# Linear attention and an ELU feed-forward on one core: batch 0 prepared in chunks of two heads, and six feature tiles open in the first product

## The chip, the cores and the metric

One core of a Trainium2 chip runs the whole program in one launch. The metric is the device time of the kernel in microseconds (us), the median over several runs. The engines named below: TensorE (PE; its weight loads are PEld), VectorE (DVE), ScalarE (ACT), GpSimd (POOL) and SyncE (SP). SP, ACT and POOL also issue DMAs[...].

## The reference

```
q, k, v: (8 batches, 8 heads, 576 rows, 64)  fp32;  g_norm: (64,)
kv  = einsum('bhsd,bhse->bhde', k, v)
out = einsum('bhsd,bhde->bhse', q, kv)
rms = sqrt(mean(out * out, axis=-1) + 1e-6)
att = out / rms * g_norm
x   = att.transpose(0, 2, 1, 3).reshape(4608, 512)
h   = x @ w_in                                # w_in  (512, 2048)
g   = where(h > 0, h, exp(min(h, 0)) - 1)
return g @ w_out                              # w_out (2048, 512), result (4608, 512) fp32
```

## The kernel before, in words

**Tiles.** The 4608 token rows are cut into nine tiles T of 512 rows. A tile's input to the feed-forward is `xT`: 128 partitions, four rows c (KC = 4) of 512 tokens. Row c, here called chunk c, is two heads; c = 2l + u, where l is the half of the partitions and u the step in which it is prepared. For one tile the first product makes 16 feature tiles of 128 (`h_ps`, two in a pair i = 0 to 7, each a sum over the four c), ELU turns them into `gT`, and the second product adds the 16 features f for four groups j of 128 tokens (`o_ps`). All matmuls are in bf16. `w_in_sb` and `w_out_sb` stay in SBUF for the whole run.

**ELU of a pair.** ACT takes Exp of the PSUM pair. DVE takes the minimum with 1 and subtracts 1, and then either takes the maximum with the PSUM pair itself, or, where ACT has also written Relu of the pair into SBUF (`relu=True`), adds that. In the first case the PSUM pair is free after DVE's pass, in the second after ACT's.

**Attention of tile 0** (the part that the diff touches). q is turned by TensorE (`turned_q`, L174) and copied to `qT`; `kv_mm` (L156) sums k and v over the rows and `kv_out` copies the result to `kv_sb`; `y_mm` (L189) gives the attention output with tokens along the free axis; ACT squares it, `mean_mm` (L199) spreads the mean over the partitions, `inv_t` takes Ln and Exp (L208, L209), and `scale_t` (L212) writes the row of `xT`. The class `Turned` does that for one u, so for two chunks at a time.

**Order.** The schedule is manual: each engine runs its instructions in the order in which the program states them. Pools give PSUM: the pairs A and B (two banks each), and two single banks each of the kinds "m" and "x"; a new tile of a kind waits until the old one is read. `idle(n)` issues n matmuls of zeros whose result nobody reads.

**The start before.** SP loads q, k and v of batch 0 in fp32, first both chunks of u = 0, then of u = 1 (six loads; the last, v of u = 1, goes into the buffer of the first q and is issued when that is cast). DVE, ACT and, for u = 1, POOL cast them to bf16 (`first_cast`). POOL's own loads begin after its casts: w_in tiles 0 to 4 in two loads (rows c = 0 and 2, then 1 and 3), its tiles 5 to 8, 9 to 12 and 13 to 15, w_out in four quarters of four f, and between these q, k, v of batches 1 and 2. At most eight of POOL's loads are under way; a further one waits for the one eight places earlier to land.

The early first product (L581) opens five feature tiles (pairs 0 and 1 and the first half of pair 2): c = 0 and 2 when u = 0 is ready, then c = 1 and 3; the other half of pair 2 follows. Pairs 3 to 7 are the regular `mm1` (L378), in "m", B, A, "x", "m"; Relu goes to ACT for pairs 2 and 6. Then the second product of tile 0 (L399) goes feature by feature over all four j, and batch 1 is prepared between its features: `mm2_all(0, 1)`, kv of batch 1 for u = 0, f = 1 and 2, q turned, f = 3 and 4, y, f = 5, means, f = 6 to 9, then the same for u = 1. w_out's third quarter is used from f = 8 on.

Of the kernel before, what the change touches and what calls it, by code (L numbers as in the profile page):

```python
# [8 lines left out]
FP32 = mybir.dt.float32  # L9
# [7 lines left out]
def kernel(  # L17
# [90 lines left out]
    def copy_on(eng, out_, in_):  # L108
        if eng is nc.scalar:
            nc.scalar.copy(out_, in_)  # L110
        else:
            eng.tensor_copy(out=out_, in_=in_)

    def load_w_in(fs, cs=slice(0, KC)):
        cols = slice(fs.start * P, fs.stop * P)
        nc.gpsimd.dma_start(  # L116
            out=w_in_sb[:, cs, cols], in_=moe_w_in.rearrange("(c p) f -> p c f", p=P)[:, cs, cols]
        )
# [24 lines left out]
    def qT_tile(b):  # L143
        qT[b] = attp.tile([P, 2, 2, RK, 64], BF16, name="qT", tag="qT", bufs=3)
        return qT[b]

    def x_tile(T):
        xT[T] = attp.tile([P, KC, G], BF16, name="xT", tag="xT")
        return xT[T]

    def kv_mm(b, kv_ps, u):
        for j in range(RK):
            for s in range(2):
                rows = slice(s * 64, s * 64 + 64)
                for l in range(2):
                    nc.tensor.matmul(  # L156
                        kv_ps[s][l * 64 : l * 64 + 64, u * 64 : u * 64 + 64],
                        lhsT=bf["k", b][rows, 2 * l + u, j, :],
                        rhs=bf["v", b][rows, 2 * l + u, j, :],
                        start=(j == 0),  # L160
                        stop=(j == RK - 1),
                    )
# [8 lines left out]
    def q_t_mm(b, u, js, dst):  # L171
        for n, j in enumerate(js):
            for l in range(2):
                nc.tensor.transpose(  # L174
                    dst[l * 64 : l * 64 + 64, n * P : n * P + P], bf["q", b][:, 2 * l + u, j, :], ident
                )

    def q_t_out(b, u, eng, src, js):
        copy_on(eng, qT[b][:, :, u, js, :], src.rearrange("p (j s r) -> p s j r", s=2, r=64))

    def y_mm(T, u, ps, ns=slice(0, 8)):

        n = ns.start
        while n < ns.stop:
            b, j = slot_of(T, n)
            m = min(ns.stop - n, RK - j)
            for l in range(2):
# [273 lines left out]

    first = {}

    def first_load(name, u, st):
        first[name, u] = st
        load(st, name, 0, slice(u, 4, 2), nc.sync)

    def first_tile(name):  # L470
        return stage.tile([P, 2, RK, D], FP32, name=f"first_{name}", tag=f"first_{name}")

    def first_cast(name, u, eng, js):
        copy_on(eng, bf[name, 0][:, u::2, js, :], first[name, u][:, :, js, :])

    low, high = slice(0, 5), slice(5, 9)
    for name in "qkv":
        bf[name, 0] = qkvp.tile([P, 4, RK, D], BF16, name=f"{name}_bf", tag=name)
        first_load(name, 0, first_tile(name))
    more = stage.tile([P, 4, RK, D], FP32, name="st_q", tag="q")  # L480
    for name, half in (("q", 0), ("k", 2)):
        first_load(name, 1, more[:, half : half + 2])
# [6 lines left out]
    nc.vector.memset(zeros, 0.0)  # L489
    nc.vector.memset(eps_col, 1e-6)  # L490
    nc.vector.memset(one, 1.0)  # L491
    nc.vector.memset(ones, 0.0)
    for l in range(2):
        nc.vector.memset(ones[l * 64 : l * 64 + 64, l * 64 : l * 64 + 64], 1.0 / D)

    idle_ps = pair("B", "idle_ps")

    def idle(n, ps=idle_ps[:, 0, :]):
        for _ in range(n):
            nc.tensor.matmul(ps, lhsT=zeros[:, 0:P], rhs=zeros, start=True, stop=True)  # L500

    def turned_q(b, u, tag):

        ps = as_bf16(single(tag, "qt_ps"))
        q_t_mm(b, u, range(8), ps)
        return ps

    qT_tile(0)
    x_tile(0)
    g_ps = pair("A", "g_ps")  # L510
    idle(9)
    nc.tensor.transpose(g_ps[:, 0, 0:1], g_row.rearrange("o l e -> o (l e)"), one)
    nc.vector.tensor_copy(out=g_col, in_=g_ps[:, 0, 0:1])
    first_cast("q", 0, V, low)
    first_cast("q", 0, A, high)
    first_load("v", 1, first_tile("q"))
    ps = turned_q(0, 0, "m")
    idle(10)
    q_t_out(0, 0, V, ps, slice(0, 8))
    first_cast("k", 0, A, high)  # L520
    first_cast("k", 0, V, low)
    first_cast("v", 0, V, low)
    first_cast("v", 0, A, high)
    kv_ps = [single("x", "kv_ps") for _ in range(2)]
    kv_mm(0, kv_ps, 0)
    idle(2)
    kv_out(0, kv_ps, 0, (V, A))
    first_cast("q", 1, V, low)
    first_cast("q", 1, Q, high)
    load_w_in(slice(0, 5), slice(0, KC, 2))  # L530
    first_cast("k", 1, Q, high)
    load_w_in(slice(0, 5), slice(1, KC, 2))
    first_cast("v", 1, Q, high)
    for lo, hi in ((5, 9), (9, 13), (13, 16)):
        load_w_in(slice(lo, hi))
    load_w_out(0)
    for name in "qkv":
# [8 lines left out]
            fetch(name, 2, u)  # L546
    fetch_ahead(3)
    cast_q(3)
    n0, n1 = Turned(0, 0), Turned(0, 1)
    y_ps = pair("A", "y_ps")  # L550
    n0.product([y_ps[:, l, :] for l in range(2)])
    for l in range(2):
        n0.square(l)
    ps = turned_q(0, 1, "m")
    q_t_out(0, 1, V, ps, slice(0, 8))
    first_cast("k", 1, V, low)
    first_cast("v", 1, V, low)
    idle(1)
    for l in range(2):
        n0.sums(l, single("x", "mean"))  # L560
        n0.inv(l)
    idle(7)
    kv_ps = pair("B", "kv_ps")
    kv_ps = [kv_ps[:, s, :] for s in range(2)]
    kv_mm(0, kv_ps, 1)
    kv_out(0, kv_ps, 1, (V, A))
    n0.scale(0)
    n0.scale(1)
    y_ps = [single("m", "y_ps") for _ in range(2)]
    idle(2, y_ps[0])  # L570
    n1.product(y_ps)
    for l in range(2):
        n1.square(l)
    g_tile(0)
    h0, h1 = pair("B", "h_ps"), pair("A", "h_ps")
    mean, h2 = single("x", "mean"), [single("x", "h_ps"), None]

    def early(h, i, a, cs):

        for c in cs:  # L580
            nc.tensor.matmul(  # L581
                h[a] if isinstance(h, list) else h[:, a, :],
                lhsT=w_in_sb[:, c, (2 * i + a) * P : (2 * i + a) * P + P],
                rhs=xT[0][:, c, :],
                start=(c == 0),
                stop=(c == KC - 1),
            )

    for a in range(2):
        early(h0, 0, a, (0,))  # L590
    n1.sums(0, mean)
    n1.inv(0)
    n1.scale(0)
    for a in range(2):
        early(h0, 0, a, (2,))
    for a in range(2):
        early(h1, 1, a, (0, 2))
    n1.sums(1, mean)
    n1.inv(1)
    n1.scale(1)  # L600
    early(h2, 2, 0, (0, 2))
    for c in (1, 3):
        for h, i, a in ((h0, 0, 0), (h0, 0, 1), (h1, 1, 0), (h1, 1, 1), (h2, 2, 0)):
            early(h, i, a, (c,))
    elu(0, 0, h0, False)()
    elu(0, 1, h1, False)()
    h2[1] = single("x", "h_ps")
    early(h2, 2, 1, (0, 2, 1, 3))
    elu(0, 2, h2, True)()
    for i, tag in zip(range(3, 8), "mBAxm"):  # L610
        mm1(0, i, tag, tag == "x")()

# [9 lines left out]

    x_tile(1)
    qT_tile(1)
    mm2_all(0, 1)
    for u in range(2):
        n = Turned(1, u)
        kv_ps = [single("x", "kv_ps") for _ in range(2)]  # L630
# [152 lines left out]
```

## Time and profile before

| | |
|---|---|
| median of 7 runs | 294.5 us (294.18 to 295.16) |
| the profiled execution | 294.84 us, of which the span from the first to the last instruction is 293.0 us |
| TensorE busy | 282.5 us, 96% of the span |
| DVE, ACT, POOL busy | 167.0, 142.1, 44.7 us |
| second product (L399), 560 matmuls of 512 columns | 130.7 us |
| first product, regular (L378), 552 such matmuls | 128.9 us |
| loads from memory | 36.70 MB |
| first regular matmul of the first product (L378) | at 21.93 us |
| matmuls of f = 8 of tile 0's second product | from 41.86 us |

A busy share is an average over stages: TensorE is full for most of the run, and the diff touches only the first 50 us, so those are read by themselves. In the profile a line "A <- B: 0.9, 1, 0.9" among the waits says that A waited for B for 0.9 us in total, once, 0.9 us at most. The chain of waits follows the work that ended last backwards; a DMA in it stands with the time from issue to landing. Stage rows give the busy time of each engine, the clock granted to TensorE, the share of the 16 DMA engines in use (it can exceed 1, as packets overlap), and the bytes written per time: a load that casts to bf16 reads twice what it writes.

### The profile page before, as it was taken

The page shows a single profiled execution, that of the slowest core. Times are in us where ns is not written, and L with a number is a line of the kernel's source. Part 1 is how long each engine was busy: PE and PEld are TensorE (multiplying, and loading weights), DVE is VectorE, ACT ScalarE, POOL GpSimd, SP SyncE. Part 2 cuts the span into 40 slices and gives each one's busy share as a digit, 9 for nine tenths or more (in the row PEclk, how much of TensorE's full clock was granted, in tenths as well). Part 3 has the DMA queues.
Part 4 walks back from the last instruction along what each step waited for, and adds up shares of the span by engine and source line. Part 5 has one row for each costly group of instructions (what it writes and reads, how often), then busy time and mean ns, then how long its engine had stood idle before and what let it go on. Part 6 is the DMA issues. An engine that isn't in the chain of part 4 may idle for free.

```text
span 293.0 us, 5198 instructions
## 1 busy us (share of the span) xinstructions
PE 282.5 (96%) x2152; PEld 129.9 (44%) x2152; DVE 167.0 (57%) x221; ACT 142.1 (48%) x210; POOL 44.7 (15%) x79
## 2 busy tenths in 40 slices
PE   7989889998999999999999999999999999999994
PEld 2434434443444444444444444444444444444443
DVE  2539723578258756774577557755775677444600
ACT  3678346678555525542554255425542554244311
POOL 0673332303300012403300330000000000000000
PEclk9999999999999999999999999999999999999999
DMA  7999999996911189968953995362331214020222
GB/s 254 280 175 206 207 205 207 316 234 192 185 34 36 27 139 245 201 88 177 254 114 71 174 255 125 63 128 72 38 81 27 72 38 104 4 74 0 72 72 74
DMA packets 46236, 38.95 MB, mean 133 GB/s; under 512 B 26372, under 2 KB 38916, under 8 KB 46212
## 3 DMA queue, kind: packets, MB, share of 16 engines
q0 software_dynamic: 14144, 19.53, 34.4%
q1 hardware_dynamic: 31664, 18.55, 29.0%
q10 hardware_dynamic: 404, 0.53, 0.5%
q8 instruction: 17, 0.28, 0.4%
q14 instruction: 7, 0.06, 0.1%
HBM read 36.70 MB, written 9.44 MB: 157 GB/s over the span
## 4 chain that ended last, share of the span: by engine, by line
PE 78%; DMA 13%; DVE 4%; ACT 2%; POOL 1%; issue 1%; DVEq 0%; SPq 0%
PE o_ps L399 37%; PE h_ps L378 35%; DMA w_out_sb<-in_moe_w_out_dram 9%; DMA xT<-xs 2%; DMA first_q<-in_v_dram 2%; DVE gT L362 2%; PE at L250 1%; PE idle_ps L500 1%; PE at L156 1%; PE o_ps L436 1%; ACT elu_e L350 1%; DVE elu_e L358 1%; POOL w_in_sb L116 1%; DVE xT L212 0%; PE qt_ps L174 0%
## 5 line engine op out<-in xcount | busy, mean ns | idle before, releaser
L399 PE MATMUL o_ps<-w_out_sb,gT 128*128 128x512 bf16 x560 | 130.7, 379 | 1.4 <-DMA w_out_sb<-in_moe_w_out_dram 0.9
L378 PE MATMUL h_ps<-xT,w_in_sb 128*128 128x512 bf16 x552 | 128.9, 379 | 1.0 <-DVE gT L362 0.8
L350 ACT ACTIVATE elu_e<-h_ps 128x1024 bf16<-128x1024 f32 (+1 forms) x77 | 73.9, 972 | 92.7 <-PE h_ps L378 89.9
L362 DVE TENSOR_TENSOR gT<-elu_e,h_ps 128x1024 bf16<-128x1024 bf16 (+1 forms) x73 | 85.6, 1177 | 7.3
L399 PEld LDWEIGHTS <-gT 128*128 128x128 bf16 x560 | 54.3, 98 | 67.6 <-issue 3.1
L378 PEld LDWEIGHTS <-w_in_sb 128*128 128x128 bf16 x552 | 52.4, 98 | 62.8 <-issue 2.1
L358 DVE TENSOR_SCALAR elu_e<-elu_e 128x1024 bf16<-128x1024 bf16 x72 | 31.5, 437 | 68.6 <-ACT elu_e L350 68.4
L415 ACT COPY o_sb<-o_ps 128x512 f32<-128x512 f32 x32 | 18.5, 588 | 18.8 <-PE o_ps L399 18.7
L103 POOL CAST q_bf<-st_q 128x384 bf16<-128x384 f32 x30 | 14.4, 530 | 28.8 <-DMA st_q<-in_q_dram 28.8
L283 DVE TENSOR_REDUCE ss<-sq 128x16 f32<-128x1024 bf16 x12 | 14.6, 1219 | 4.9 <-ACT sq L277 4.9
L212 DVE SCALAR_TENSOR_TENSOR xT<-y_ps,g_col,rT 128x512 bf16<-128x512 f32 x12 | 8.9, 749 | 15.0 <-ACT rT L209 15.0
L299 DVE TENSOR_TENSOR xs<-at,ss 128x1024 bf16<-128x1024 f32 x12 | 14.6, 1217 | 0.0
L277 ACT ACTIVATE sq<-at 128x1024 bf16<-128x1024 f32 x12 | 12.3, 1028 | 1.0 <-PE at L250 1.0
L339 POOL COPY gate<-qT 1x32 bf16<-1x32 bf16 x4 | 0.8, 202 | 72.6 <-DMA qT<-q_bf 72.6
L229 ACT ACTIVATE sq<-y_ps 128x512 bf16<-128x512 f32 x12 | 6.5, 595 | 7.8 <-PE y_ps L189 7.8
L500 PE MATMUL idle_ps<-zeros 128*128 128x512 bf16 x29 | 9.0, 458 | 1.2 <-DVE one L491 1.2
L208 ACT ACTIVATE rT<-mean,eps_col 128x512 f32<-128x512 f32 x12 | 8.2, 683 | 1.7 <-PE mean L199 1.5
L156 PEld LDWEIGHTS <-k_bf 64*64 64x64 bf16 x576 | 5.7, 107 | 5.7 <-issue 5.2
L209 ACT ACTIVATE rT<-rT 128x512 f32<-128x512 f32 x12 | 7.6, 630 | 0.4
L90 POOL DMA_DIRECT2D k_bf<-in_k_dram x9 | 6.6, 738 | 5.6 <-DMA w_in_sb<-in_moe_w_in_dram 1.8
L90 POOL DMA_DIRECT2D v_bf<-in_v_dram x9 | 6.7, 743 | 4.2 <-DMA w_out_sb<-in_moe_w_out_dram 1.8
L312 DVE TENSOR_SCALAR xT<-xT,g_col 128x1024 bf16<-128x1024 bf16 x12 | 5.8, 479 | 2.7 <-DMA xT<-xs 2.7
(59 smaller groups left out, 97.6 us busy)
## 6 DMA issues: line engine op xcount, KB each, us to landing
out_dram<-o_sb SPq DMA_DIRECT2D x24, 256.0 KB, 4.0
st_q<-in_q_dram POOLq DMA_DIRECT2D x5, 1152.0 KB, 7.8
k_bf<-in_k_dram POOLq DMA_DIRECT2D x5, 576.0 KB, 10.5
v_bf<-in_v_dram POOLq DMA_DIRECT2D x5, 576.0 KB, 14.3
out_dram<-o_sb SPq DMA_DIRECT2D x19, 128.0 KB, 2.6
w_out_sb<-in_moe_w_out_dram POOLq DMA_DIRECT2D x4, 512.0 KB, 14.0
q_bf<-in_q_dram POOLq DMA_DIRECT2D x4, 288.0 KB, 14.1
k_bf<-in_k_dram POOLq DMA_DIRECT2D x4, 288.0 KB, 14.2
```

The costliest lines, as they stand in the source:

```text
L90: eng.dma_start(out=dst.rearrange("p m j d -> p m (j d)"), in_=in_[:, ms, :])
L103: nc.gpsimd.tensor_copy(out=bf["q", b][:, u, js], in_=raw[b][:, u::2, js, :].rearrange("p l j d -> p j l d"),)
L277: nc.scalar.activation(sq, st["se", h], AF.Square)
L283: nc.vector.reduce_sum(out=ss, in_=st.pop(("sq", h)).rearrange("p l (m e) -> p (l m) e", e=D), axis=AX.X,)
L299: nc.vector.tensor_tensor(out=st["xs"][:, 2 * h : 2 * h + 2, :].rearrange("p i (l m e) -> p l i m e", l=2, e=D), in0=se_ps.rearrange("p l ...
L350: nc.scalar.activation(e[:, lo:hi, :], h, AF.Exp)
L358: nc.vector.tensor_scalar(out=e, in0=e, scalar1=1.0, scalar2=1.0, op0=ALU.min, op1=ALU.subtract)
L362: nc.vector.tensor_tensor(out=gT[T][:, 2 * i + lo : 2 * i + hi, :], in0=e[:, lo:hi, :], in1=h, op=ALU.add if relu else ALU.max,)
L378: nc.tensor.matmul((ps[a] if isinstance(ps, list) else ps[:, a, :])[:, cols], lhsT=w_in_sb[:, c, f * P : f * P + P], rhs=xT[T][:, c, cols] ...
L399: nc.tensor.matmul(o_ps[T, j], lhsT=gT[T][:, f, j * P : j * P + P], rhs=w_out_sb[:, f, :], start=(f == 0), stop=(f == FC - 1),)
L415: nc.scalar.copy(o_sb[T, half][:, j % 2, :], o_ps[T, j])
L500: nc.tensor.matmul(ps, lhsT=zeros[:, 0:P], rhs=zeros, start=True, stop=True)
```

## The change

Batch 0 is now prepared chunk by chunk. SP issues three loads only: q of chunks 0 and 2, k of chunk 0, v of chunk 0, in fp32. Everything else of batch 0 is loaded by POOL straight into the bf16 tiles, from its first DMA on, in the order k2, v2, q1 with q3, k1, v1, w_in row 0 of tiles 0 to 5, k3, v3, w_in rows 2, 1 and 3 of the same tiles, then w_in tiles 6 and 7, 8 to 11, 12 to 15; the rest of the list stays. What is left to cast at the start are the three loads of SP: DVE makes two casts (before: six), ACT three as before, POOL none (before: three).

`kv_mm` and `y_mm` take a list of the halves l, so that one chunk can be done alone. Chunks 0 and 2 share one Ln and Exp of 1024 elements; chunks 1 and 3 each have their own Ln, and Exp and scale in halves of 256 tokens. The idle matmuls are placed anew: 8, 6, and then ones, threes and fours between the steps, 26 in all (before: 9, 10, 2, 1, 7, 2, that is 31).

The early product opens all six feature tiles of pairs 0 to 2 (in "x", B and A) and does their last row, c = 3, at the end, tile by tile; ELU of the three pairs follows. The regular pairs 3 to 7 take "m", "x", B, A, "m"; Relu goes to ACT for pairs 1, 4, 5 and 6. The call of `mm2_all(0, 1)` is split in two, with the same order of its matmuls. Nothing changes after that.

```diff
-    def kv_mm(b, kv_ps, u):
+    def kv_mm(b, kv_ps, u, ls=range(2)):
...
-                for l in range(2):
+                for l in ls:
...
-    def y_mm(T, u, ps, ns=slice(0, 8)):
+    def y_mm(T, u, ps, ls=range(2)):
...
+    first = {"q": first_load("q", (0, 2)), "k": first_load("k", (0,)), "v": first_load("v", (0,))}
...
+    def chunk_load(name, cs):
+        ms = slice(cs[0], cs[-1] + 1, 2)
+        load(bf[name, 0][:, ms], name, 0, ms)
+
+    chunk_load("k", (2,))
+    chunk_load("v", (2,))
+    chunk_load("q", (1, 3))
+    chunk_load("k", (1,))
+    chunk_load("v", (1,))
+    load_w_in(slice(0, 6), slice(0, 1))
+    chunk_load("k", (3,))
+    chunk_load("v", (3,))
+    for c in (2, 1, 3):
+        load_w_in(slice(0, 6), slice(c, c + 1))
+    for lo, hi in ((6, 8), (8, 12), (12, 16)):
         load_w_in(slice(lo, hi))
...
+    def chunk_kv(kv_ps, c):
+        kv_mm(0, [kv_ps[:, s, :] for s in range(2)], c % 2, (c // 2,))
+
+    def chunk_kv_out(kv_ps, c, eng):
+        rows, cols = slice(c // 2 * 64, c // 2 * 64 + 64), slice(c % 2 * 64, c % 2 * 64 + 64)
+        copy_on(eng, kv_sb[rows, 0, c % 2], kv_ps[rows, :, cols])
...
+    def chunk_y(c, ps):
+        y_ps[c] = ps
+        y_mm(0, c % 2, {c // 2: ps}, (c // 2,))
+
+    def chunk_square(c):
+        sq0[c] = attp.tile([P, G], BF16, name="sq", tag="sq")
+        nc.scalar.activation(sq0[c], y_ps[c], AF.Square)
+
+    def chunk_scale(c, r, cols=slice(0, 512)):
+        scale_t(0, y_ps[c][:, cols], r[:, cols], c, cols)
+
+    def chunk_norm(c, mean):
+
+        r = r_tile()[:, 0, :]
+        nc.scalar.activation(r, mean, AF.Ln, bias=eps_col)
+        for n in range(2):
+            cols = slice(n * 256, n * 256 + 256)
+            nc.scalar.activation(r[:, cols], r[:, cols], AF.Exp, scale=-0.5)
+            chunk_scale(c, r, cols)
...
+    idle(8, kv_ps[:, 0, :])
...
+    ps = turned_q(0, 0, "m")
+    idle(6, kv_ps[:, 0, :])
+    first_cast("k", (0,), A, slice(0, RK))
+    q_t_out(0, 0, V, ps, slice(0, 8))
+    first_cast("v", (0,), A, high)
+    first_cast("v", (0,), V, low)
+    mean = pair("A", "mean")
+    chunk_kv(kv_ps, 0)
+    chunk_kv_out(kv_ps, 0, V)
+    chunk_kv(kv_ps, 2)
+    chunk_kv_out(kv_ps, 2, V)
+    chunk_y(0, single("x", "y_ps"))
+    chunk_square(0)
+    idle(1, mean[:, 0, :])
+    chunk_y(2, single("x", "y_ps"))
+    chunk_square(2)
+    idle(1, mean[:, 0, :])
+    mean_mm(sq0[0], mean[:, 0, :])
+    idle(1, mean[:, 1, :])
+    mean_mm(sq0[2], mean[:, 1, :])
+    r = r_tile()
+    inv_t(r, mean)
+    ps = turned_q(0, 1, "m")
+    q_t_out(0, 1, V, ps, slice(0, 8))
+    y1 = single("m", "y_ps")
+    idle(3, y1)
+    kv_ps = pair("B", "kv_ps")
+    chunk_kv(kv_ps, 1)
+    chunk_kv_out(kv_ps, 1, V)
+    idle(1, y1)
+    chunk_y(1, y1)
+    chunk_square(1)
+    chunk_scale(0, r[:, 0, :])
+    chunk_scale(2, r[:, 1, :])
+    mean = pair("A", "mean")
+    idle(4, mean[:, 1, :])
+    mean_mm(sq0[1], mean[:, 0, :])
+    h_ps = [pair("x", "h_ps")]
+    early([(0, 0)], 0)
+    idle(1, mean[:, 1, :])
+    early([(0, 1)], 0)
+    chunk_kv(kv_ps, 3)
+    chunk_kv_out(kv_ps, 3, V)
+    chunk_norm(1, mean[:, 0, :])
+    early([(0, 0)], 2)
+    y3 = single("m", "y_ps")
+    chunk_y(3, y3)
+    chunk_square(3)
+    h_ps.append(pair("B", "h_ps"))
+    early([(1, 0), (1, 1)], 0)
+    early([(0, 1)], 2)
+    mean_mm(sq0[3], mean[:, 1, :])
+    chunk_norm(3, mean[:, 1, :])
+    early([(1, 0), (1, 1)], 2)
+    early([(0, 0), (0, 1), (1, 0), (1, 1)], 1)
+    h_ps.append(pair("A", "h_ps"))
+    for c in (0, 2, 1):
+        early([(2, 0), (2, 1)], c)
+    early([(i, a) for i in range(3) for a in range(2)], 3)
+    for i in range(3):
+        elu(0, i, h_ps[i], i == 1)()
+    for i, tag in zip(range(3, 8), "mxBAm"):
+        mm1(0, i, tag, i in (4, 5, 6))()
...
-    mm2_all(0, 1)
+    for js in ((2, 3), (0, 1)):
+        mm2_all(0, 1, js)
```

More of the change, by code (lines that the diff above doesn't have):

```diff
@@ L179, in q_t_out @@
         copy_on(eng, qT[b][:, :, u, js, :], src.rearrange("p (j s r) -> p s j r", s=2, r=64))
-    def y_mm(T, u, ps, ns=slice(0, 8)):
-        n = ns.start
-        while n < ns.stop:
+    def y_mm(T, u, ps, ls=range(2)):
+        n = 0
+        while n < 8:
             b, j = slot_of(T, n)
-            m = min(ns.stop - n, RK - j)
-            for l in range(2):
+            m = min(8 - n, RK - j)
+            for l in ls:
                 for s in range(2):
@@ L460, in store, with first_load @@
                 nc.sync.dma_start(out=rows[b1][:, j1, :], in_=o[hs, 1, :])
[L464 to L474, printed above, removed]
+    def first_load(name, cs):
+        st = stage.tile([P, len(cs), RK, D], FP32, name=f"first_{name}", tag=f"first_{name}")
+        load(st, name, 0, slice(cs[0], cs[-1] + 1, 2), nc.sync)
+        return st
     low, high = slice(0, 5), slice(5, 9)
@@ L478 @@
         bf[name, 0] = qkvp.tile([P, 4, RK, D], BF16, name=f"{name}_bf", tag=name)
[L479 to L482, printed above, removed]
+    first = {"q": first_load("q", (0, 2)), "k": first_load("k", (0,)), "v": first_load("v", (0,))}
     g_row = const.tile([1, 2, 64], FP32, name="g_row")
@@ L487 @@
     make_identity(nc, ident)
[L489 to L534, printed above, removed]
+    def chunk_load(name, cs):
[12 more added lines that the diff above has]
+    for lo, hi in ((6, 8), (8, 12), (12, 16)):
         load_w_in(slice(lo, hi))
@@ L548 @@
     cast_q(3)
-    n0, n1 = Turned(0, 0), Turned(0, 1)
-    y_ps = pair("A", "y_ps")
-    n0.product([y_ps[:, l, :] for l in range(2)])
+    nc.vector.memset(zeros, 0.0)
+    nc.vector.memset(eps_col, 1e-6)
+    nc.vector.memset(one, 1.0)
+    nc.vector.memset(ones, 0.0)
     for l in range(2):
[L553 to L580, printed above, removed]
+        nc.vector.memset(ones[l * 64 : l * 64 + 64, l * 64 : l * 64 + 64], 1.0 / D)
@@ new lines, in idle, with turned_q, first_cast @@
+    def idle(n, ps):
+        for _ in range(n):
+            nc.tensor.matmul(ps, lhsT=zeros[:, 0:P], rhs=zeros, start=True, stop=True)
+    def turned_q(b, u, tag):
+        ps = as_bf16(single(tag, "qt_ps"))
+        q_t_mm(b, u, range(8), ps)
+        return ps
+    def first_cast(name, cs, eng, js):
+        copy_on(eng, bf[name, 0][:, cs[0] : cs[-1] + 1 : 2, js, :], first[name][:, :, js, :])
+    def chunk_kv(kv_ps, c):
+        kv_mm(0, [kv_ps[:, s, :] for s in range(2)], c % 2, (c // 2,))
@@ new lines, in chunk_kv_out @@
+    def chunk_kv_out(kv_ps, c, eng):
+        rows, cols = slice(c // 2 * 64, c // 2 * 64 + 64), slice(c % 2 * 64, c % 2 * 64 + 64)
+        copy_on(eng, kv_sb[rows, 0, c % 2], kv_ps[rows, :, cols])
+    y_ps, sq0 = {}, {}
+    def chunk_y(c, ps):
[6 more added lines that the diff above has]
+        scale_t(0, y_ps[c][:, cols], r[:, cols], c, cols)
@@ L581, in early @@
+    def chunk_norm(c, mean):
[5 more added lines that the diff above has]
+            chunk_scale(c, r, cols)
+    def early(tiles, c):
+        for i, a in tiles:
+            h = h_ps[i]
             nc.tensor.matmul(
@@ L587, in early @@
             )
[L589 to L611, printed above, removed]
+    qT_tile(0)
+    x_tile(0)
+    g_tile(0)
+    g_ps = pair("A", "g_ps")
+    kv_ps = pair("B", "kv_ps")
+    idle(8, kv_ps[:, 0, :])
+    nc.tensor.transpose(g_ps[:, 0, 0:1], g_row.rearrange("o l e -> o (l e)"), one)
+    nc.vector.tensor_copy(out=g_col, in_=g_ps[:, 0, 0:1])
+    first_cast("q", (0, 2), V, low)
+    first_cast("q", (0, 2), A, high)
@@ new lines @@
+    mean_mm(sq0[0], mean[:, 0, :])
[7 more added lines that the diff above has]
+    idle(3, y1)
+    kv_ps = pair("B", "kv_ps")
+    chunk_kv(kv_ps, 1)
[7 more added lines that the diff above has]
+    idle(4, mean[:, 1, :])
```

## The prediction

> **What bounds the kernel now.** I read the page first, then the waits of TensorE in the first 70 us, then the chain of waits up to 45 us, then busy time and DMA rate by stage. On the page, the rows of slices:
>
> ```profile
> span 293.0 us, 5198 instructions
> ...
> PE   7989889998999999999999999999999999999994
> ...
> DMA  7999999996911189968953995362331214020222
> ...
> PE 78%; DMA 13%; DVE 4%; ACT 2%; POOL 1%; issue 1%; DVEq 0%; SPq 0%
> ```
>
> TensorE is full except in the first six slices (44 us) and the last. In those slices the DMA row is full too, and the chain that ends last has 13% of DMA in it. So the diff, which only touches the start, must be judged against two clocks: TensorE's own work and the stream of loads. Who held TensorE, from its waits:
>
> ```profile
> PE kv_ps L156 <- DMA v_bf<-in_v_dram: 0.9, 1, 0.9
> PE o_ps L399 <- DMA w_out_sb<-in_moe_w_out_dram: 0.9, 1, 0.9
> ...
> PE h_ps L581 <- DVE xT L212: 0.6, 2, 0.3
> PE h_ps L581 <- DMA w_in_sb<-in_moe_w_in_dram: 0.3, 1, 0.3
> ```
>
> and the chain up to 45 us (start, length, what):
>
> ```profile
> 6.08 6.27 DMA first_q<-in_v_dram
> ...
> 13.35 2.16 POOL w_in_sb L116 x3
> 15.51 12.58 DMA w_out_sb<-in_moe_w_out_dram
> ...
> 28.37 13.44 DMA w_out_sb<-in_moe_w_out_dram
> ...
> 41.86 1.89 PE o_ps L399 x8
> ```
>
> The reader is to see that from 6 us to 41.86 us the chain is loads, not arithmetic: the third quarter of w_out lands at 41.81, and the matmul with f = 8 waits for it although TensorE was done with f = 7 at 40.98. From 41.86 on the chain is TensorE. Whatever the change gains counts as far as the f = 8 matmul starts before 41.86, and no further. The stream by stage (columns: PE, PEld, DVE, ACT, POOL busy, clock, DMA share, GB/s written):
>
> ```profile
> 3.00:11.50 8.50, 7.67 (x94) 3.38 (x93) 3.49 (x8) 3.15 (x6) 1.97 (x4) 1.00 1.04 397
> 11.50:17.50 6.00, 5.67 (x62) 2.50 (x61) 2.87 (x7) 5.10 (x10) 5.92 (x9) 1.00 0.97 130
> 17.50:41.50 24.00, 21.84 (x154) 9.49 (x153) 14.69 (x24) 15.20 (x26) 9.58 (x14) 1.00 1.23 205
> ```
>
> First fp32 into SBUF (bytes read = bytes written, 397 GB/s), later fp32 cast to bf16 (205 written = 410 read). Between them is a hole: 130 GB/s for 6 us, that is 6.0 x (205 - 130)/205 = 2.2 us of stream lost. There GpSimd has only just begun to issue: it cast q first (9.41), and its three casts stand between its first w_in loads.
>
> **The change part by part.**
>
> *The load stream.* SP now issues 1.18 MB (q of chunks 0 and 2, k and v of chunk 0) instead of 3.54 MB; GpSimd issues the rest of batch 0 as casting loads from about 1.4 us, with no cast between its issues. At 0.70 to 0.86 us of issue each, eight are out by 7.5 us; the ninth waits for the first to land, as now (the chain: w_out's third load goes out at 28.37, once its first, eight issues earlier, has landed at 28.08). SP has nothing queued behind its three loads until 50 us. The q load of batch 3, which shared a buffer with the first loads and waited for DVE until 42.42, now waits for a landing only: earlier, and in nobody's way. Bytes read are the same (w_in reaches 6 tiles earlier, 0.26 MB). If GpSimd is ahead, the hole closes and everything behind it comes 2.2 us earlier: v of batch 1 at 30.3 instead of 32.5, w_out's third quarter at 39.6 instead of 41.81. Bounds: 0 (the hole stays, wherever it moves) to 2.8 (the two queues overlap without loss); I take 2.2, what the hole itself cost.
>
> *A rule against it.* The row: 205 GB/s in 17.5 to 41.5 us with pieces of 288 to 512 KB, eight in flight. The Trainium skill, "DMA: Bandwidth & Descriptors", section "Bandwidth", says to batch to 1 MiB or more, and its section on the SWDGE path gives some 2.0 us fixed plus bytes / 436 GB/s for one DMA. By the rule the eleven pieces of 144 to 288 KB up to the last early w_in piece are a loss: 2.0 us each is 22 us if they ran singly, and with eight in flight some 3 us. By the row the fixed part is hidden as soon as several are queued. I follow the row; 3 us stays as the bad end (stream 0.8 us late).
>
> *When v of chunk 0 lands.* Now q lands at 4.86 and v at 7.87, SP's loads alone. After the change both queues are filled. Nearest row, where both are full (57 to 61 us):
>
> ```profile
> q0 software_dynamic: 383, 0.42, 61.3%
> q1 hardware_dynamic: 380, 0.68, 52.0%
> ```
>
> Packet for packet they share evenly. SP's part is 512 packets of 2304 B; alone they go at about 176 per us (397 GB/s), shared at about 90. About 70 go alone until 3.2 us, the other 444 take 4.9 us: 8.1, plus 0.8 us from the last packet to the wake-up (as v's 768 packets from 2.6 us end near 7.0 and land at 7.87): 8.9 us. Bounds 7.3 (SP goes first) and 10.5 (SP gets a third). q lands at 6.1 by the same count.
>
> *The chain to xT*, from v at 8.9, with the durations of now. Cast of 256 elements on ACT 0.39 (between 0.21 for 64 and 0.62 for 512), kv matmuls at 9.45, copy out at 9.9 (0.26), y at 10.3, squares 0.60 each at 10.8 and 11.3, the second mean at 11.95, Ln on 1024 elements 1.1 (0.69 + 512 more at 0.43, as Exp's 0.60 to 1.02), Exp 1.06, the two scales end at 15.3 and 16.05 (now 14.81 and 15.46). Chunk 1: y at 14.3, square, mean at 15.4, Ln 0.69, Exp and scale in halves: 17.9. Chunk 3: kv copy out at 16.8, behind both scales on DVE; y at 17.2, square ends 18.25, mean 18.3, Ln 19.4, Exp halves, last scale ends 20.8 (now 19.63). The k, v and w_in pieces for these steps come 2 us or more ahead. TensorE has 18 early matmuls to do meanwhile; the last six (row c = 3, spacing 0.216) run from 21.15 to 22.45. Now the first regular matmul (L378) starts at 21.93: 0.5 us later, though 0.3 us of waiting for w_in's tile 5 (21.06) is gone. The kernel's idle matmuls (26 for 31) lie in gaps and cost nothing unless cold.
>
> *ELU.* Three banks finish together and four tiles use Relu (1, 4, 5, 6) instead of two (2, 6). ACT runs from 21.55 in one piece: Exp pairs at 0.92 to 0.96, five of one kind and three of the other, four Relu at 0.92 to 0.96: Relu of tile 6 ends at 31.95. Banks for tiles 4 to 7 are free in time (DVE drops two of its 1.22 us PSUM passes for 0.69 us ones). 40 matmuls end at 22.45 + 40 x 0.216 = 31.05; w_out's first two go into B, the two into A wait for that Relu, 0.5 us (now they also wait 0.5): kv of batch 1 could start at 32.45. Now it starts at 32.54, after 0.9 us of waiting for v, which then is there since 30.3. The split of the call for f = 0 keeps the order of its four matmuls: nothing.
>
> *To f = 8.* From there 40.98 - 32.54 = 8.44 us of work, unchanged: 40.9. The quarter of w_out is there at 39.6. So f = 8 starts at 40.9 instead of 41.86: 0.95 us earlier. Behind it nothing is removed or added, later loads only come earlier, and the last quarter (landing near 46.4 now, used after 47.5) moves with the stream.
>
> *Sum.* The profiled execution took 294.84, of it 293.0 span; less 0.95 is 293.9. It stood 0.34 over the median of 294.5, so the forecast is about 293.5.
>
> *A second rule, on the clock.* The row of the idle matmuls (PE busy, PEld busy, clock, DMA share, GB/s):
>
> ```profile
> 1.19:5.21 4.02, 4.02 (x9) 1.20 (x9) 1.00 0.83 254
> 6.63:8.96 2.33, 2.33 (x10) 0.89 (x10) 1.00 1.05 393
> ```
>
> The first nine run at 0.43 us each, the next ten at 0.22, though the clock column says 1.00 both times. The Trainium skill, "TensorE: Matmul & The Clock Gate", Part 1, says that the array is at half rate until a window of about 3.4 us was busy, and that the window runs free. It speaks against the change: eight idle matmuls (3.4 us) for nine, and then a gap until q is turned at 6.85 (now 6.06). By the row the second group runs at 0.22; by the rule the six idle matmuls may take 2.6 us instead of 1.3 and end at 10.1, which moves kv from 9.45 to 10.1: 0.65 us of the 0.95 gone. I take the row, and keep the rule's end in the range.
>
> **The rivals.**
>
> *The stream does not move.* The hole may come from casting loads being slow to get going, not from their late issue; then it costs 2.2 us wherever they start. For it: the first w_in loads took 5.1 to 7.7 us to land. Against: the share of 0.97 at 130 GB/s has gaps between the loads, and now SP's loads cover the start. Then f = 8 waits for 41.8 as now: 294.5, no change.
>
> *SP's loads go first.* If GpSimd's first descriptors come at 4 us or later, v lands near 7.9, the chain is 1 us shorter, TensorE reaches f = 8 at 39.9, and w_out at 39.6 to 39.9 is the bound: gain about 2, 292.4. For it: the first casting load came some 1.5 us after its issue, when SP's were all but over. Against: 57 to 61 us shows an even split.
>
> *The clock stays cold (slower).* Place: from the turning of q (6.85) into the early product. Price: 0.65 us for the six idle matmuls, 0.1 to 0.2 us for each y and mean on the chain, 0.2 us for each early matmul. It decides from about 13 us on: cold until then costs some 1.6 us (0.7 slower); cold until 17 us some 2.5: 296.0. For it: eight for nine, and the longer gap. Against: idle matmuls fill 7.5 to 8.8, which alone should warm it by 10 or 11 us.
>
> **How the numbers follow.** About 0.2% (0.6 us) is what a measurement of this kernel can tell from no change. Chances: my forecast 0.45 (292.9 to 294.0, nearly all of it faster); SP first 0.17 (292.2 to 292.8); stream unmoved, or v late by a further 0.5 to 1 us, 0.18 (294 to 295); cold clock or small pieces starving 0.20 (295.1 to 297). So faster 0.61, same 0.19, slower 0.20. The range 292.2 to 295.5 leaves out the worse half of the slow case and a little below.
>
> **What would show it.** Right: DMA rate without a stage of 130 GB/s before 20 us; v of chunk 0 waking ACT near 8.9; last scale near 20.8; L378 starting near 22.4; a wait of L399 for ACT near 31.5; no wait of TensorE for v_bf or w_out_sb. Wrong: idle matmuls at 0.43 us after 7 us (cold); w_out_sb still ending the wait of L399 near 41.8 (stream unmoved); L378 starting after 23.5 (chain longer than reckoned).

## The result, and the profile after

The changed kernel takes 293.53 us (median of 14 runs, 291.98 to 294.07); the kernel before, in the same comparison, 294.77 us (34 runs, 293.98 to 295.7). The ratio is 0.9951, 95% interval 0.9939 to 0.9964: faster by about half a per cent. The 14 times are not spread evenly: four lie at 291.98 to 292.49 and ten at 293.37 to 294.07. (A fifteenth run on record, which the median does not count, took 292.94 and lies between the two groups.) The profiled execution, 293.63 us with a span of 291.9 us, belongs to the larger group. What separates the two groups turns out to be half of this case.

The page of the changed kernel: the span, TensorE and DMA in 40 slices, and the shares of the chain by engine.

```profile
span 291.9 us, 5185 instructions
...
PE   7999999998999999999999999999999999999994
...
DMA  7999999998711189948944896352331214020222
...
PE 90%; DVE 4%; ACT 3%; DMA 1%; issue 1%; DVEq 0%
```

The loads have left the chain: 1% DMA where it was 13%. TensorE's waits in the first 70 us agree: neither w_out nor v nor w_in appears among them any more:

```profile
PE h_ps L378 <- DVE gT L362: 0.9, 2, 0.5
...
PE o_ps L399 <- ACT elu_h L354: 0.4, 1, 0.4
PE kv_ps L156 <- DVE kv_sb L112: 0.4, 1, 0.4
PE o_ps L399 <- DVE gT L362: 0.3, 1, 0.3
```

The stream by stage (PE, PEld, DVE, ACT, POOL busy, clock, DMA share, GB/s written):

```profile
3.00:11.50 8.50, 7.23 (x69) 2.98 (x67) 2.13 (x6) 2.21 (x4) 5.94 (x11) 1.00 1.12 251
11.50:17.50 6.00, 5.94 (x73) 2.71 (x71) 2.44 (x5) 4.12 (x6) 4.59 (x7) 1.00 1.23 201
17.50:41.50 24.00, 23.54 (x164) 10.45 (x164) 14.58 (x28) 17.47 (x32) 8.69 (x12) 1.00 1.23 206
```

The hole of 130 GB/s at 11.5 to 17.5 us is gone (201). The first row is lower than before (251 for 397) because casting loads write half of what they read.

The start, from the timeline (start, length, engine, line, what, and in brackets the idle time before it and who ended it):

```profile
1.19 3.59 PE L519 MATMUL kv_ps<-zeros 128*128 128x512 bf16 x8 [1.19 <-DVE one L512]
...
5.91 1.07 PE L174 MATMUL qt_ps<-ident,q_bf 128*64 128x128 bf16 x16 [0.72 <-DVE q_bf L112]
6.91 2.60 PE L519 MATMUL kv_ps<-zeros 128*128 128x512 bf16 x6
...
7.19 0.40 ACT L110 CAST v_bf<-first_v 128x256 bf16<-128x256 f32 x1 [0.90 <-DMA first_v<-in_v_dram]
...
9.43 0.47 PE L156 MATMUL kv_ps<-v_bf,k_bf 64*64 64x64 bf16 x18
...
10.28 0.38 PE L156 MATMUL kv_ps<-v_bf,k_bf 64*64 64x64 bf16 x13 [0.38 <-DVE kv_sb L112]
...
20.47 0.87 DVE L212 SCALAR_TENSOR_TENSOR xT<-y_ps,g_col,rT 128x256 bf16<-128x256 f32 x2 [1.60 <-ACT rT L556]
22.99 8.80 PE L378 MATMUL h_ps<-xT,w_in_sb 128*128 128x512 bf16 x40
...
32.60 0.59 PE L399 MATMUL o_ps<-w_out_sb,gT 128*128 128x512 bf16 x2 [0.39 <-ACT elu_h L354]
...
39.67 3.62 PE L399 MATMUL o_ps<-w_out_sb,gT 128*128 128x512 bf16 x16
```

v of chunk 0 is there at 7.19, but kv starts only at 9.43: TensorE still works on six idle matmuls, at 0.43 us each. In what follows TensorE is called cold where a matmul of 512 columns takes 0.43 us and warm where it takes 0.22. The last 16 matmuls are f = 7 and f = 8 in one piece, so f = 8 starts at 39.67 + 8 x 0.216 = 41.40 (before: 41.86), not held by a load.

### The profile page after: what moved, and what is told of

Its sections match the earlier page's. It is cut to its first block, busy times and chain, and to the rows that moved or that the text cites. A ratio compares the mean times of both kernels' runs of the same rounds, so it can differ in the third digit from the quotient of the medians.

```text
span 291.9 us, 5185 instructions
## 1 busy us (share of the span) xinstructions
PE 283.6 (97%) x2147; PEld 130.5 (45%) x2147; DVE 165.4 (57%) x222; ACT 143.0 (49%) x209; POOL 47.0 (16%) x85
## 4 chain that ended last, share of the span: by engine, by line
PE 90%; DVE 4%; ACT 3%; DMA 1%; issue 1%; DVEq 0%
PE o_ps L399 40%; PE h_ps L378 38%; DVE gT L362 2%; ACT elu_e L350 2%; PE h_ps L563 2%; PE at L250 2%; DMA g_row<-in_g_norm_dram 1%; PE qt_ps L174 1%; PE at L156 1%; PE o_ps L436 1%; PE kv_ps L519 1%; PE kv_ps L156 1%; DVE elu_e L358 1%; PE mean L199 1%; PE y_ps L189 1%; PE mean L519 1%
## 5 line engine op out<-in xcount | busy, mean ns | idle before, releaser
L378 PE MATMUL h_ps<-xT,w_in_sb 128*128 128x512 bf16 x552 | 128.7, 379 | 1.1 <-DVE gT L362 0.9
L362 DVE TENSOR_TENSOR gT<-elu_e,h_ps 128x1024 bf16<-128x1024 bf16 (+1 forms) x72 | 83.3, 1161 | 7.1
L378 PEld LDWEIGHTS <-w_in_sb 128*128 128x128 bf16 x552 | 52.3, 98 | 62.7 <-issue 2.0
L212 DVE SCALAR_TENSOR_TENSOR xT<-y_ps,g_col,rT 128x512 bf16<-128x512 f32 (+1 forms) x14 | 9.2, 671 | 14.4 <-ACT rT L209 12.5
L90 POOL DMA_DIRECT2D k_bf<-in_k_dram x12 | 8.5, 709 | 5.6 <-DMA w_out_sb<-in_moe_w_out_dram 2.1
L90 POOL DMA_DIRECT2D v_bf<-in_v_dram x12 | 8.3, 690 | 5.5 <-DMA w_in_sb<-in_moe_w_in_dram 1.8
L156 PEld LDWEIGHTS <-k_bf 64*64 64x64 bf16 x576 | 6.3, 107 | 5.8 <-issue 5.8
L229 ACT ACTIVATE sq<-y_ps 128x512 bf16<-128x512 f32 x8 | 4.3, 595 | 6.5 <-PE y_ps L189 6.5
L208 ACT ACTIVATE rT<-mean,eps_col 128x512 f32<-128x512 f32 (+1 forms) x9 | 6.6, 731 | 1.8 <-PE mean L199 1.6
L519 PE MATMUL kv_ps<-zeros 128*128 128x512 bf16 x14 | 6.2, 618 | 1.2 <-DVE one L512 1.2
L112 DVE COPY qT<-qt_ps 128x128 bf16<-128x128 bf16 (+1 forms) x10 | 3.7, 406 | 5.4 <-PE qt_ps L174 5.4
```

The lines of the kernel that those rows point to most:

```text
L156: nc.tensor.matmul(kv_ps[s][l * 64 : l * 64 + 64, u * 64 : u * 64 + 64], lhsT=bf["k", b][rows, 2 * l + u, j, :], rhs=bf["v", b][rows, 2 * ...
L362: nc.vector.tensor_tensor(out=gT[T][:, 2 * i + lo : 2 * i + hi, :], in0=e[:, lo:hi, :], in1=h, op=ALU.add if relu else ALU.max,)
L378: nc.tensor.matmul((ps[a] if isinstance(ps, list) else ps[:, a, :])[:, cols], lhsT=w_in_sb[:, c, f * P : f * P + P], rhs=xT[T][:, c, cols] ...
```

## The experiments

Times beside "before" are those of the runs of the kernel before on the same chip.

**1. Warm: two more idle matmuls ahead of the turning of q.**

```diff
+    idle(2, kv_ps[:, 0, :])
     ps = turned_q(0, 0, "m")
     idle(6, kv_ps[:, 0, :])
```

> The changed kernel with two more idle matmuls just before q of chunk 0 is turned, so that TensorE is busy without a gap from 1.2 us on. In the profile of the changed kernel the six idle matmuls after q's turning ran at 0.43 us each and kv of chunk 0 started behind them at 9.43. Clock theory (the array is still at half rate there, and in the quicker runs of the changed kernel it is not): with more work ahead the six run at 0.22, kv starts near 8.1 to 8.3, the whole is about 1.1 us shorter than the changed kernel's usual 293.5, near 292.4. Rival (the six are slow for another reason, such as the loads): kv at 9.4 to 9.6 as before, 293.5 to 293.7.

Measured: 292.27 us (six runs, 292.16 to 292.96), before 294.84, ratio 0.9919 (0.9902 to 0.9936). More work at the start, and no run lies in the upper group any more; one of the six, 292.96, lies between the groups. Its timeline:

```profile
6.16 1.47 PE L519 MATMUL kv_ps<-zeros 128*128 128x512 bf16 x6
7.56 0.47 PE L156 MATMUL kv_ps<-v_bf,k_bf 64*64 64x64 bf16 x18
...
21.11 8.80 PE L378 MATMUL h_ps<-xT,w_in_sb 128*128 128x512 bf16 x39
...
39.84 1.89 PE L399 MATMUL o_ps<-w_out_sb,gT 128*128 128x512 bf16 x8 [0.15 <-DMA w_out_sb<-in_moe_w_out_dram]
```

The six take 1.47 us, kv starts 1.87 us earlier than in the profile of the changed kernel, L378 1.88 us earlier, and f = 8 now meets w_out's third quarter again, at 39.84.

**2. Cold: four idle matmuls at the very start instead of eight.**

```diff
-    idle(8, kv_ps[:, 0, :])
+    idle(4, kv_ps[:, 0, :])
```

> The changed kernel with four idle matmuls instead of eight at the very start, nothing else. If the two groups of times of the changed kernel (292.0 to 292.5 and 293.4 to 294.1) come from whether TensorE is already at full rate when the six idle matmuls begin: 1.7 us of idle work is not enough, no run is warm, and every run lies at 293.4 to 294.1, the six idle matmuls take 2.6 us, the first regular L378 starts near 23.0. If the groups have another cause (the loads, for instance): runs near 292 stay among them, about a third.

Measured: 294.16 us (12 runs, 293.45 to 296.1), before 295.02, ratio 0.9982 (0.9962 to 1.0002), so no longer clear of the kernel before. No run is below 293.45, so the lower group has vanished, as expected if the clock makes the groups. But the times also go above the band that it gave: two runs at 294.4 and 294.71 and three at 295.66 to 296.1. The profiled run (293.87) is of the ordinary cold kind, its six idle matmuls in one piece:

```profile
6.71 2.74 PE L519 MATMUL kv_ps<-zeros 128*128 128x512 bf16 x6
```

That the slowest three stayed cold for longer still would fit, but is not shown: none of them was profiled.

**3. The changed kernel once more, unchanged.**

> The changed kernel, unchanged, profiled once more. If the clock's phase is chance: either as in the first profile (the six idle matmuls 2.6 us, first regular L378 at 23.0, total near 293.6), or warm (1.3 to 1.5 us, L378 near 21.1 to 22.1, total 292.0 to 292.5), and the total goes with which of them it is. If the clock does not make the two groups: the total and the duration of the six do not go together.

Measured: 292.09 us, one run, and its trace is the warm one:

```profile
6.47 1.47 PE L519 MATMUL kv_ps<-zeros 128*128 128x512 bf16 x6
7.87 0.47 PE L156 MATMUL kv_ps<-v_bf,k_bf 64*64 64x64 bf16 x18
...
21.42 8.82 PE L378 MATMUL h_ps<-xT,w_in_sb 128*128 128x512 bf16 x40
...
38.11 3.75 PE L399 MATMUL o_ps<-w_out_sb,gT 128*128 128x512 bf16 x16
```

One and the same kernel: kv starts at 7.87 or at 9.43, L378 at 21.42 or at 22.99, and the total is 1.54 us apart. The 1.56 us at kv are the slower turning of q and the slower idle matmuls (q is turned at 5.9 in both). With experiments 1 and 2 this shows that the clock makes the two groups. Nothing in the program decides which of them a run falls into: eight idle matmuls (1.19 to 4.78 us) and then 1.1 us with one small matmul in it, until q is turned, are sometimes enough and sometimes not.

**4. Fewer idle matmuls between q and kv: two instead of six.**

```diff
-    idle(6, kv_ps[:, 0, :])
+    idle(2, kv_ps[:, 0, :])
```

> The changed kernel with two idle matmuls instead of six after q of chunk 0 is turned. v of chunk 0 was there at 7.19 and cast by 7.95 while the six held TensorE until 9.4. If only their number counts: kv at 8.0, 1.3 us shorter than the changed kernel, 292.2. Clock theory: kv starts at 8.0 as well, but the array stays at half rate for longer; the means, y and above all the matmuls of the early product from 15 us on then take 0.43 us, which gives back most of it or more: 293.2 to 295.

Measured: 293.93 us (12 runs, 291.97 to 294.84), before 294.84, ratio 0.9964 (0.9945 to 0.9982). No gain over the changed kernel. kv starts 1.44 us earlier, but the array stays cold for longer:

```profile
7.99 0.69 PE L156 MATMUL kv_ps<-v_bf,k_bf 64*64 64x64 bf16 x18
...
10.59 0.64 PE L189 MATMUL y_ps<-qT,kv_sb 64*64 64x512 bf16 x2 [0.47 <-DVE kv_sb L112]
...
12.41 0.63 PE L199 MATMUL mean<-sq,ones 128*128 128x512 bf16 x1
...
23.36 8.80 PE L378 MATMUL h_ps<-xT,w_in_sb 128*128 128x512 bf16 x39
```

kv 0.69 for 0.47, y 0.64 for 0.40, the mean 0.63 for 0.38; the second mean is 0.12 us later than with six, and L378 0.37 later. So in these two cold profiles the six idle matmuls that delay kv also pay for themselves.

**5. The loads alone.** The kernel before, with its attention by u unchanged, but q, k, v of u = 1 loaded by GpSimd's casting loads (so that their casts fall away) and w_in directly behind them.

```diff
-    more = stage.tile([P, 4, RK, D], FP32, name="st_q", tag="q")
-    for name, half in (("q", 0), ("k", 2)):
-        first_load(name, 1, more[:, half : half + 2])
...
+    for name in "qkv":
+        load(bf[name, 0][:, 1::2], name, 0, slice(1, 4, 2))
+    load_w_in(slice(0, 5), slice(0, KC, 2))
+    load_w_in(slice(0, 5), slice(1, KC, 2))
...
-    first_load("v", 1, first_tile("q"))
...
-    first_cast("q", 1, V, low)
-    first_cast("q", 1, Q, high)
...
```

> The kernel before with the load half of the change alone: q, k, v of u = 1 are loaded by GpSimd straight into bf16 from its first DMA on, and w_in's first two loads follow at once; no chunks, the product as before. If the earlier stream is what gains: no stage at 130 GB/s, w_out's third quarter lands at 39.6 to 40.3, and the time falls by 0.9 us against before, to 293.8. If the chunking is needed with it: SP still loads 1.77 MB before the first y and shares the engines with GpSimd's loads, v of u = 0 lands 1 to 2 us later than 7.87, the chain to the first product moves by as much, and the time is that of before, 294.3 to 295.

Measured: 293.5 us (12 runs, 292.75 to 295.86), before 294.84, ratio 0.9965 (0.9945 to 0.9985). The expectation that the chunks are needed as well fell, although v did land 1.1 us later, as it said. On the median this half is as good as the whole change; by the ratio it brings about 0.7 of it (0.35% beside 0.49%), and the two intervals overlap. It closes the hole, from its stages and its chain:

```profile
11.50:17.50 6.00, 5.60 (x60) 2.42 (x62) 2.23 (x4) 5.21 (x11) 2.18 (x3) 1.00 1.20 203
```

```profile
1.75 7.24 DMA first_v<-in_v_dram
```

Its profiled run, 293.06 us, was warm, with v landing at 8.99 and L378 at 22.24.

**6. The loads alone, and warm.**

```diff
+    idle(2)
     ps = turned_q(0, 0, "m")
```

> The kernel before with its loads alone changed (u = 1 of batch 0 and then w_in by GpSimd's casting loads), and two idle matmuls more before q is turned, so that TensorE is warm by then. It asks what the chunks bring when the clock is no longer in play. If chunking by two heads is worth what separates the warm changed kernel (292.27) from the loads alone (293.06 in its profile): 293.0 to 293.5, v at 9.0, first L378 near 22.2. If chunking brings nothing and the clock was all: 292.3.

Measured: 293.69 us (seven runs, 293.42 to 294.1), before 295.02, ratio 0.9953 (0.9936 to 0.997). Two more idle matmuls bring nothing here beside experiment 5 (ratio 0.9965). Beside the warm changed kernel (292.27, ratio 0.9919) the chunks, together with the rest of the change (six open feature tiles, the ELU and the idle matmuls placed anew), are worth 1.0 us by the two ratios, 1.4 by the medians, when the clock is warm in both. How much of it is the chunks' own was not tried. From its chain and its timeline:

```profile
1.75 8.10 DMA first_v<-in_v_dram
```

```profile
10.41 0.48 PE L156 MATMUL kv_ps<-v_bf,k_bf 64*64 64x64 bf16 x36 [1.24 <-DVE v_bf L112]
```

Here TensorE waits for v: SP loads three times 0.59 MB before it has everything, and v lands at 9.85 (8.99 in experiment 5, with the same loads; why it differs stays open). L378 starts at 23.10. Both are later than expected (9.0 and 22.2), and so is the time. With chunks SP loads only two thirds of that, and v lands at 7.19. In a cold run this lead is wasted, since kv waits for the idle matmuls until 9.43. This fits that the loads alone reach the same median.

**7. kv of chunk 2 in a PSUM pair of its own**, so that it does not wait for DVE's copy of chunk 0.

```diff
-    mean = pair("A", "mean")
+    kv2_ps = pair("A", "kv2_ps")
...
-    chunk_kv(kv_ps, 2)
-    chunk_kv_out(kv_ps, 2, V)
+    chunk_kv(kv2_ps, 2)
+    chunk_kv_out(kv2_ps, 2, V)
+    mean = pair("A", "mean")
```

> The changed kernel with kv of chunk 2 summed in PSUM banks of its own (the pair A, before the means take it), instead of the pair that holds chunk 0. In the changed kernel TensorE waited 0.38 us at 10.28 for DVE's copy of chunk 0 before it began chunk 2. If that wait is on the chain: kv of chunk 2 right behind chunk 0, second y near 10.8 instead of 11.2, all later steps 0.35 us earlier, 293.2. If the chain is held by something else (squares, Ln): within 0.1 us of the changed kernel, 293.5.

Measured: 292.38 us (six runs: four at 292.19 to 292.5, two at 293.24 and 293.47), before 294.84, ratio 0.9927 (0.9908 to 0.9946). The low median only says that four of six runs fell into the low group, and they don't beat that of the changed kernel (291.98 to 292.49). The profiled one (293.24) was cold: the wait of 0.38 is gone, but from the start of kv to the second mean it takes 12.13 - 9.31 = 2.82 us, against 12.29 - 9.43 = 2.86. In this run kv itself was still cold (36 matmuls in 0.99 us), which may hide a part of the gain. Behind it the two squares stand one behind the other on ACT and set the time of the second mean (changed kernel first, then this one):

```profile
10.98 1.26 ACT L545 ACTIVATE sq<-y_ps 128x512 bf16<-128x512 f32 x2 [3.39 <-PE y_ps L189]
...
12.29 0.38 PE L199 MATMUL mean<-sq,ones 128*128 128x512 bf16 x1
```

```profile
10.82 1.25 ACT L545 ACTIVATE sq<-y_ps 128x512 bf16<-128x512 f32 x2 [3.59 <-PE y_ps L189]
...
12.13 0.38 PE L199 MATMUL mean<-sq,ones 128*128 128x512 bf16 x1
```

**8. The kernel before, with w_out's third quarter loaded earlier.** Is the wait before f = 8 really the limit?

```diff
     load_w_out(1)
+    load_w_out(2)
     for name in "qkv":
         fetch(name, 1, 1)
-    for s in (2, 3):
-        load_w_out(s)
+    load_w_out(3)
```

> The kernel before with one load moved: the third quarter of w_out is issued ahead of q, k, v of batch 1's u = 1. Its wait of 0.88 us before f = 8 was counted as the limit of any gain at the start. If that wait costs its full length: f = 8 at 40.98, no wait for w_out_sb, 0.9 us faster than before (about 293.9 beside 294.8). If the wait only moves (k and v of batch 1, u = 1 land 1.4 us later and TensorE waits for them between f = 8 and f = 12): no gain, 294.8.

Measured: 294.22 us (12 runs, 293.38 to 294.49), before 295.0, ratio 0.9968 (0.9954 to 0.9981). One line moved brings some 0.8 us, over half of what the change brings. f = 8 starts at 40.81 instead of 41.86 without a wait for w_out, and no wait for k or v comes in its place. Of the 1.05 us gained there, part is given back far behind (all from its timeline):

```profile
39.08 3.61 PE L399 MATMUL o_ps<-w_out_sb,gT 128*128 128x512 bf16 x16
...
126.12 0.49 DVE L312 TENSOR_SCALAR xT<-xT,g_col 128x1024 bf16<-128x1024 bf16 x1 [1.28 <-DMA xT<-xs]
...
128.32 1.89 PE L378 MATMUL h_ps<-xT,w_in_sb 128*128 128x512 bf16 x8 [0.56 <-DVE gT L362]
```

**9. The kernel before once more, unchanged.**

> The kernel before, unchanged, profiled once more. In its first profile DVE waited 0.91 us at 126.6 for the transposed xT and the first product followed late; in the changed kernel's profile there was no such wait, worth 0.35 us of the difference. If the wait belongs to the order of the loads of the kernel before: it is there again, 0.8 to 1.0. If it is a chance of the single run (0, 0.18, 0.31, 0.41 and 0.77 were seen in profiles of variants): it is smaller, anything from 0.

Measured: 295.73 us, one run. The wait at 127.35 is there again (0.89), so it is not a chance of one run of this kernel. And the early waits are longer:

```profile
PE o_ps L399 <- DMA w_out_sb<-in_moe_w_out_dram: 1.5, 1, 1.5
PE h_ps L581 <- DMA w_in_sb<-in_moe_w_in_dram: 1.3, 1, 1.3
```

with 116 GB/s instead of 130 in the hole. f = 8 starts at 42.80, 0.94 us later than in the first profile, and the total is 0.89 us longer. The depth of the hole thus differs between these two runs, and the difference is found again in their times.

**10. and 11. A better version, in two steps from experiment 1.** First kv of batch 1 is put between the two halves of f = 0, where TensorE waited for Relu; then w_out's third quarter goes ahead of batch 1's u = 1 as in experiment 8.

```diff
-    for js in ((2, 3), (0, 1)):
-        mm2_all(0, 1, js)
+    mm2_all(0, 1, (2, 3))
...
+            mm2_all(0, 1, (0, 1))
```

> The changed kernel, warm (two idle matmuls more before q is turned), with kv of batch 1 moved between the two halves of f = 0, so that TensorE does not wait 0.39 us for Relu before bank A's groups of f = 0. If f = 8 is bound by the third quarter of w_out (its wait was 0.15 at 39.84): no gain, 292.0 to 292.5, the wait for w_out_sb grows to about 0.5. If TensorE's own chain still counts there: 0.39 faster, 291.9.

Measured: 292.12 us (six runs, 292.04 to 292.37), before 295.02, ratio 0.9901 (0.9882 to 0.992). The wait for Relu is gone, but the time is that of experiment 1 within the intervals. In its profiled run q was still turned cold (1.06 us for 0.64) in spite of the ten idle matmuls ahead of it, and only the six behind it were warm (1.48 us); L378 started at 22.07 and f = 8 at 40.13, so it doesn't show the longer wait for w_out that I expected; whether w_out takes the gain stays undecided by this run.

```diff
+    load_w_out(2)
     for name in "qkv":
         fetch(name, 1, 1)
-    for s in (2, 3):
-        load_w_out(s)
+    load_w_out(3)
```

> The kernel of the run before it, with the third quarter of w_out issued ahead of q, k, v of batch 1's u = 1 instead of behind them. If the third quarter bounds f = 8 there: no wait for w_out_sb, f = 8 at 39.45, 291.6 to 291.9. A rival: k and v of batch 1, u = 1, now land 1.4 us later, and kv of u = 1 after f = 8 to 10 or y waits for them: 292.0 to 292.5.

Measured: 291.77 us (six runs, 291.33 to 292.43), before 295.02, ratio 0.9891 (0.9872 to 0.9911), the fastest of all. f = 8 starts at 37.55 + 1.73 = 39.28 with no wait:

```profile
1.19 3.27 PE L519 MATMUL kv_ps<-zeros 128*128 128x512 bf16 x8 [1.19 <-DVE one L512]
...
21.22 8.80 PE L378 MATMUL h_ps<-xT,w_in_sb 128*128 128x512 bf16 x40
...
37.55 3.61 PE L399 MATMUL o_ps<-w_out_sb,gT 128*128 128x512 bf16 x16
```

No wait for k or v of batch 1 shows either. Here the last of the first eight idle matmuls already ran at the higher rate (3.27 us for the eight, 3.59 in the changed kernel). The step from 292.12 to 291.77 is small against the overlap of the two intervals; the whole way from the changed kernel is not.

## Why the prediction was right or wrong

The predicted 293.5 us stands beside 293.53 measured. That the two agree so closely is luck: the load stream came as reckoned, but two large errors in the path to kv cancelled, the path behind kv was put 0.5 us too short, and what was lost there came back far behind, in the profiled executions, by something that the sum did not have. By the medians the gain is 1.24 us (294.77 to 293.53); the forecast, from 294.5, was 1.0.

*The load stream: right.* The hole closed. w_out's third quarter, put at 39.6, has landed by 40.3, where the issue of the next load ends its wait for it; the warm runs place it at about 39.8. Experiment 8 confirms what made it matter: the wait of 0.88 us before f = 8 did cost about its length (some 0.8 us by the medians). *The rule of 1 MiB against the small pieces: the row held.* Pieces of 144 to 288 KB wrote 204 to 206 GB/s from 7 to 10 us, and no step to xT waited for them.

*When v of chunk 0 lands: wrong, 8.9 predicted, 7.19 measured.* The step that failed is "about 70 go alone until 3.2 us". GpSimd's first load was issued at 1.45 us, but its packets come only from 4.7 us. The queues of the changed kernel, 1.4 to 4.5 us (packets, MB, share of the engines):

```profile
q1 hardware_dynamic: 321, 0.71, 80.0%
```

and 4.5 to 7.2 us:

```profile
q0 software_dynamic: 288, 0.31, 66.0%
q1 hardware_dynamic: 239, 0.47, 48.7%
```

SP's queue had 60% of its 512 large packets through alone. From there the two did share about evenly, as the row of 57 to 61 us said. So the rival "SP's loads go first" was right in its condition, GpSimd later than 4 us.

*The six idle matmuls: wrong, 1.3 us predicted, 2.60 in the profile.* I took the row of the kernel before (0.22 each) and kept the Trainium skill's rule ("TensorE: Matmul & The Clock Gate", Part 1) for the range. Taking the row was the step that failed: the rule's end came true in most runs. The traces fit the rule's window that runs free: the same kernel is warm in one run and cold in another (experiment 3), and after the same first eight idle matmuls from 1.19 us on TensorE was warm before 4.5 us in experiment 11, only behind the turning of q (7.1 us) in experiment 10, and at about 9.4 us in the profile of the changed kernel. How long the window is, no run here measures. The row had come from a run after nine idle matmuls (4.02 us) and a shorter gap.

*The two together:* v 1.7 us early, the idle matmuls 1.3 us longer and ending last: kv started at 9.43, predicted 9.45.

*The chain to xT: 0.5 us too short.* The second mean came at 12.29 instead of 11.95: my sum let the second square start 0.5 us after the first, but they run one behind the other on ACT, 1.26 us for both, and the first began 0.2 us late. The rest comes at chunk 3. I let the copy of its kv wait for DVE's two scales alone and put it at 16.8. It came at 17.45, for TensorE reached that kv only at 16.93, behind chunk 1's mean (15.98) and the early matmuls:

```profile
17.45 0.29 DVE L112 CAST kv_sb<-kv_ps 64x128 bf16<-64x128 f32 x1 [1.10 <-PE kv_ps L156]
```

The last scale ended at 21.34 (20.8), L378 began at 22.99 (22.45).

*ELU and bank A: right.* A wait of 0.39 us for Relu at 32.60 (0.5 predicted), and kv of batch 1 without its wait for v, at 33.12 (32.45). (40 x 0.216 from 22.45 on is 31.09 and not 31.05; nothing hangs on that.)

*To f = 8: half the gain, 0.46 us instead of 0.95.* And "behind it nothing is removed or added" was not quite so. In the profile before, DVE waited 0.91 us at 126.60 for the transposed xT, and the first product followed 0.18 us late; in the profile after there is no such wait. Before:

```profile
126.60 0.48 DVE L312 TENSOR_SCALAR xT<-xT,g_col 128x1024 bf16<-128x1024 bf16 x1 [0.91 <-DMA xT<-xs]
...
128.80 1.46 PE L378 MATMUL h_ps<-xT,w_in_sb 128*128 128x512 bf16 x6 [0.18 <-DVE gT L362]
```

After:

```profile
125.37 0.48 DVE L312 TENSOR_SCALAR xT<-xT,g_col 128x1024 bf16<-128x1024 bf16 x1
126.27 3.62 PE L378 MATMUL h_ps<-xT,w_in_sb 128*128 128x512 bf16 x16
```

From there on TensorE is 0.81 us ahead instead of 0.46, and the rest of the 1.1 us by which the spans differ lies behind the last matmul. So the profiled executions differ by 294.84 - 293.63 = 1.21 us where 0.95 was summed, by another road. The 0.35 us does not depend on the load order alone: three runs of the order of before had this wait (0.91, 0.89, 1.28), but of the new order some had it too (0.67 in experiment 3, 0.77 in experiment 1), where TensorE lost only 0.1 and 0.2 us by it (16 matmuls in 3.72 and 3.81 us for 3.62). What the transposes collide with was not tried.

*The rivals.* In a warm run "SP's loads go first" came out nearly as worked: f = 8 at 39.9 and w_out the bound there, 292.4 predicted, 291.98 to 292.49 measured. "The clock stays cold" is what most runs show in its mild form, and experiment 2 has runs at its 296.0, of which none was profiled. My forecast's number lies where most runs do because both held at once.

## What to carry to other kernels

When idle work is to warm TensorE, leave no gap between it and the first real matmuls, and look at several runs to see whether it is long enough: here two more idle matmuls (some 0.6 us in an otherwise empty gap) were worth 0.9 us by the ratios (1.3 by the medians) and made the time steady, though in experiment 10 even they did not warm TensorE before q was turned. Earlier data buys nothing while the engine that uses it is held by something else, so look at which of the two ends last before counting a gain. And a load whose landing alone sets a point of the chain may simply be moved ahead of loads that are used later, before anything is rebuilt.

## What the runs showed of the hardware that was not expected

- The granted clock of the profile says 1.00 both when a matmul of 512 columns takes 0.43 us and when it takes 0.22. Only the spacing of the idle matmuls tells the two apart.
- The first casting loads of GpSimd move nothing until 3.3 us after their first issue at the kernel's start (1.45 to 4.7 us in the changed kernel).
- The times of one and the same program on one core can fall in two groups, some 1.5 us apart, by the rate at which TensorE runs in the first 10 us (experiment 3).
- When the first rows of w_in load in the changed kernel, the written rate dips to between 120 and 180 GB/s for some 1.5 us (10.5 to 12 us) and then recovers, with single packets taking up to 0.34 us instead of 0.13. Its cause stays open; TensorE did not wait for it there.
